# A second batch's attention woven into the first batch's groups: steps planned by a search, and steps from a fixed table

## The chip, the cores and the metric

The kernel runs on one core of one Trainium2 chip. Its metric is the device time of one execution in microseconds (us), the median of several runs. In this text TensorE is PE in the profile (PEld is its weight load), VectorE is DVE, ScalarE is ACT, GpSimd is POOL and SyncE, which issues the DMAs, is SP.

## What is computed

Agent attention for two batches, then a feed-forward layer with a learned slope, cut here to what matters:

```
# q, k, v: (2, 12480, 128); agents: (2, 49, 128)
def sm(a, b):
    s = scale * (a @ b.transpose(0, 2, 1))
    s = s - s.max(-1, keepdims=True)
    e = np.exp(s)
    return e / (e.sum(-1, keepdims=True) + 1e-09)
agent_v = sm(agents, k) @ v            # per batch: needs all keys and values
x = (sm(q, agents) @ agent_v).reshape(24960, 128)
h = x @ w_in                           # w_in: (128, 2048)
g = np.maximum(h, 0) + alpha * np.minimum(h, 0)
out = g @ w_out                        # w_out: (2048, 128)
```

## The kernel before

Queries are taken in 52 groups of 480 (26 a batch), and each group in 8 steps, so there are 416 steps; two groups make a pair of 16 steps. A step s first issues the matmuls of `h` for step s + 2 (`g1`: six, L824, then ScalarE's `rh` = relu, L830, and VectorE's `rl` = the rest that `rh` rounds off, L831), then whatever the plan holds for step s, then twelve matmuls that add `rh` and `rl` into `acc` (`g2`, L846). All are 480 columns wide and use half of the rows each, two side by side. `h` has two buffers, so the matmuls of `h` for step s + 2 overwrite what `rl` of step s reads. `acc` has two banks, one for even and one for odd groups; whatever else TensorE computes during a group (`pair_tile`) uses the bank of the other group, between the read-out of the last group and the start of the next. At the end of a group `acc` goes through `os` (L862, L863), is transposed at the next group's step 1 (`o_take`, L868), scaled (`o_scale`, L873) and stored (`o_store`).

Each pair of groups also has its query chain (`q_transpose` to `q_rec`), on fixed steps, among them the query logits at the pair's step 2 (`q_logits`, L740), GpSimd's all-reduce that follows (`q_max`, L753) and the sums at step 4 (`q_sum`).

The first batch's keys and values are done ahead of step 0. Those of the second batch must be done, and folded with `w_in` into `sab` and with the linear part into `zh`, `zl`, by step 208, where its groups begin; they are woven into the first batch's steps. Keys come in 25 units of 512: a load (`load_kb`, four DMAs on SP), a transposition on VectorE (`kt`, L366), a burst of sixteen small float32 matmuls for two units (`k_logits`, L384), a copy on ScalarE and an addition on VectorE (`k_take`), and a maximum (`k_max_keys`, L423). After all of them `k_max` joins the maxima. Values follow: subtract the maximum (`k_exp_a`, L507), exponentials (`k_exp_b`), the low part (`k_exp_c`, L526), the values' two parts (`v_split`, L497, L498, with a memset on GpSimd), a burst of matmuls (`k_av2`, L572) and an addition (`k_add`, L582). Then the fold: `t1` divides by the denominator, `t2` turns the result, four `ta` multiply it with a quarter of `w_in` each, `tz` and `ts` make `zh` and `zl`.

Before, a search puts all that on steps: `fit` gives VectorE and ScalarE budgets a step (`ROOM`, L21), `hold` finds two free steps for a bank (L1026), and each unit goes to the first step that has room (L1060 to L1119). The code below shows it; the order of the code inside a step is the order of the engines' queues, and each engine takes its queue strictly in that order.

Of the kernel before, what the change touches and what calls it, by code (L numbers as in the profile page):

```python
# [13 lines left out]
ALU = mybir.AluOpType  # L14
# [3 lines left out]
WORD_LO = 2.0**-15  # L18
WORD_HI = 122880.0

ROOM = {"dve": 1.4, "act": 1.1}  # L21


CUTS = (3, 8, 15, 21)
# [7 lines left out]
def kernel(  # L32
# [11 lines left out]
    nc = tc.nc  # L44
    B, N, C = q.shape
# [8 lines left out]
    NG = N // GT  # L54
    KT = 512
    UB = KT // P
    NU = -(-N // KT)
    NKB = NU * UB
    W = 512
# [4 lines left out]
    NM = NF // 2  # L64
# [39 lines left out]
    win = const.tile([P, DFF], F32, name="win")  # L104
# [485 lines left out]
    def fold_tasks(b):  # L590
        w = st[b]

        rows = w["rows"]
        parts = rows // NA
# [31 lines left out]
            t = big(b, "sab", F32R)  # L626
            w["sa"], w["sb"] = t[:, 0:DFF], t[:, DFF : 2 * DFF]

        def ta(n):
            def f():  # L630
                t = pair_tile(f"a_ps{b}_{n}", 0 if b == 0 and n == 1 else None)[:, 0, :]
                sl = slice(n * W, (n + 1) * W)
                nc.tensor.matmul(t, lhsT=w["avt"], rhs=win[:, sl], start=True, stop=True)
                nc.scalar.copy(out=w["sa"][:, sl], in_=t)
                nc.vector.tensor_tensor(
                    out=w["sb"][:, sl], in0=t, in1=w["sa"][:, sl], op=ALU.subtract
                )

            return f

# [58 lines left out]
    NGT = B * NG  # L699
# [193 lines left out]
    with tc.manual_schedule():  # L893
# [7 lines left out]
        for b in range(B):  # L901
# [3 lines left out]
            out=oma, in0=alp, scalar1=-1.0, scalar2=1.0, op0=ALU.mult, op1=ALU.add  # L905
# [7 lines left out]
        def at(s, f, *a):  # L913
            plan.setdefault(s, []).append((f, a))
# [9 lines left out]
        s = 0  # L924
# [78 lines left out]
            at(4, f)  # L1003

        q_steps = (-20, -19, -18, -14, -13, -13, -10, -7, -6, -5, 4, 5, 10)
        load = {}

        first = {}

        def pre(s, f, *a):  # L1010
            first.setdefault(s, []).append((f, a))

        def use(s, eng, cost):
            load[eng, s] = load.get((eng, s), 0.0) + cost

        def fit(s, **costs):

            while any(load.get((e, s), 0.0) + c > ROOM[e] for e, c in costs.items()):
                s += 1
            for e, c in costs.items():  # L1020
                use(s, e, c)
            return s

        busy = set()

        def hold(s):  # L1026

            while s in busy or s + 1 in busy or s % NM in (0, 1, NM - 1):
                s += 1
            busy.update((s, s + 1))  # L1030
            return s

        for i2 in range(NGT // 2):
            s0 = 2 * NM * i2
            if i2 == 0:
                at(10, q_sum, 0)
                pre(11, q_spread, 0)
                at(13, q_rec, 0)
                busy.update((0, 1, 2, 3, 4, 5, 6, 7, 10, 11))
# [6 lines left out]
            for i in (3, 10):  # L1046
                busy.update((s0 + steps[i], s0 + steps[i] + 1))
            for f, i in zip(q_chain, steps):
                (pre if f in (q_take, q_spread) else at)(s0 + i, f, i2)
        for g in range(NGT):  # L1050
            s0 = g * NM
            for i in range(NM):
                use(s0 + i, "dve", 0.57)
            for i in (7, 7, 0, 1):
                use(s0 + i, "act", 0.5)
# [4 lines left out]
        for b in range(1, B):  # L1060
            base = (b - 1) * NG * NM
            parts = [(u, u + 2) for u in range(0, NU - 3, 2)] + [(NU - 3, NU)]
            assert NU % 2
            at(base + 8, k_begin, b, [(0, NU)], parts)
            s = base + 9
            done, used = {}, {}
            for c, (lo, hi) in enumerate([*parts[:-1], (NU - 3, NU - 1), (NU - 1, NU)]):
                us = tuple(range(lo, hi))
                for u in us:
                    s = fit(max(s, done.get(u - 3, 0) + 1), dve=0.57)  # L1070
                    at(max(base, s - 9, used.get(("k", u - 3), 0) + 1), load_kb, b, u)
                    used["k", u] = s
                    at(s, k_transpose_dve, b, u)
                    s += 1
                t_log = hold(max(s + 1, done.get(lo - 1, 0) + 2))
                done.update((u, t_log) for u in us)
                at(t_log, k_logits, b, us)
                pre(t_log + 1, k_take, b, us)
                use(t_log + 1, "dve", 0.4)
                if hi in (NU, *(p[1] for p in parts)):  # L1080
                    t_max = fit(t_log + 2, dve=0.4)
                    at(t_max, k_max_keys, b, min(c, len(parts) - 1))
            s = t_max + 1
            at(s, k_max, b)
            s += 3
            done = {}
            for lo, hi in parts:
                us = list(range(lo, hi))
                t_av = s
                for u in us:  # L1090
                    s = fit(s, dve=0.3)
                    at(s, k_exp_a, b, u)
                    t_v = fit(max(s, done.get(u - 4, 0) + 1), act=0.5, dve=0.57)
                    at(max(base, t_v - 8, used.get(("v", u - 3), 0) + 1), load_v1, b, u)
                    used["v", u] = t_v
                    at(t_v, v_split, b, u)
                    t_e = fit(max(s + 1, done.get(u - 4, 0) + 1), act=0.5)
                    at(t_e, k_exp_b, b, u)
                    t_c = fit(t_e + 1, dve=0.3)
                    at(t_c, k_exp_c, b, u)  # L1100
                    t_av = max(t_av, t_c + 2, t_v + 2)
                t_av = hold(t_av)
                at(t_av, k_av2, b, us)
                pre(t_av + 1, k_add, b, us)
                use(t_av + 1, "dve", 0.5)
                for u in us:
                    done[u] = t_av
            s = t_av + 2
            at(s, k_sum, b)
            lead, rest = fold_tasks(b)  # L1110
            s += 2
            for f in lead:
                s = hold(s)
                at(s, f)
                s += 2
            s = hold(s)
            at(s, rest[0])
            at(s + 1, rest[1])
            s += 2  # L1119
            assert s < base + (NG + 1) * NM - 1, (t_max, t_av, s, base + NG * NM)  # L1120

        for s in range(NS):
            step[0] = s
# [40 lines left out]
```

## Time and profile before

| | us |
|---|---|
| median of 3 runs (lowest, highest) | 1036.93 (1036.47, 1040.59) |
| the profiled execution | 1038.73 |
| its span, first to last instruction | 1037.0 |
| TensorE busy | 1015.8 (98%) |
| VectorE busy | 818.2 (79%) |
| ScalarE busy | 630.5 (61%) |
| GpSimd busy | 112.7 (11%) |

Busy shares are means over stages that differ: the stage ahead of step 0 ends near 92 us, the second batch's work lies between 110 and 600 us, and behind it the groups run alone. Matmuls are pipelined and their ends are modelled, so a wait of TensorE shows first in the starts of its instructions and in its weight loads. What the views name by line is the code above; the names of the tiles stand behind the lines.

### The profile page before, as it was taken

Reading aid. Unit: us, or ns where it says so; the run is one execution under the profiler, and the core shown is the slowest. Engines: PE = TensorE matmul, PEld = TensorE weight load, DVE = VectorE, ACT = ScalarE, POOL = GpSimd, SP = SyncE. Lnnn points to the kernel's source line nnn. Section 1 sums busy time; section 2 is a strip of 40 time slices with the busy share of each in tenths; the row PEclk is TensorE's granted clock in tenths of the full one; section 3 lists DMA queues with packets and bytes.
Section 4 is the critical chain, followed back from the end, with each engine's and each line's share of the span. In section 5 each row is a group of like instructions: output and inputs, shape, how many; then the busy total and the mean of one; then the engine's idle time right before and its main releaser. Section 6 shows DMA issues by size and latency. Waiting matters only on the chain.

```text
span 1037.0 us, 22307 instructions
## 1 busy us (share of the span) xinstructions
PE 1015.8 (98%) x9263; PEld 935.2 (90%) x9263; DVE 818.2 (79%) x1040; ACT 630.5 (61%) x801; POOL 112.7 (11%) x138
## 2 busy tenths in 40 slices
PE   9899999999999999999999999999999999999997
PEld 7786888988988888999888799999999998999997
DVE  6966778878878899988977777787778777887775
ACT  4355556656656576777755665666666665666563
POOL 3341110010011011011011011101110011101100
PEclk9899999999999999999999999999999999999999
DMA  9963034324332222332220211121112111211011
GB/s 297 290 131 50 14 51 67 53 44 67 52 49 36 61 63 59 70 79 54 59 35 12 39 30 19 32 40 30 26 24 39 31 33 19 39 30 21 11 20 30
DMA packets 295045, 57.22 MB, mean 55 GB/s; under 512 B 265567, under 2 KB 292769, under 8 KB 294945
## 3 DMA queue, kind: packets, MB, share of 16 engines
q1 hardware_dynamic: 293953, 55.69, 26.8%
q8 instruction: 72, 1.18, 0.5%
q10 hardware_dynamic: 992, 0.12, 0.1%
q14 instruction: 28, 0.23, 0.1%
HBM read 42.59 MB, written 12.78 MB: 53 GB/s over the span
## 4 chain that ended last, share of the span: by engine, by line
PE 79%; DVE 13%; ACT 3%; issue 2%; DMA 1%; SPq 1%; DVEq 0%; ACTq 0%
PE acc L846 43%; PE h L824 22%; DVE rl L831 4%; PE lg L740 3%; PE kl L384 3%; ACT rh L830 2%; PE av L539 2%; PE acc L857 1%; DVE qt L718 1%; PE qsum L782 1%; DVE ql L730 1%; DMA qin<-in_q_dram 1%; DVE kt L366 1%; PE ktp L352 1%; ACT qh L725 1%
## 5 line engine op out<-in xcount | busy, mean ns | idle before, releaser
L831 DVE SCALAR_TENSOR_TENSOR rl<-h,rh 128x960 fp32r<-128x960 f32 x416 | 478.7, 1152 | 184.4 <-ACT rh L830 181.0
L830 ACT ACTIVATE rh<-h 128x960 fp32r<-128x960 f32 x416 | 404.5, 972 | 288.4 <-PE h L824 282.9
L824 PE MATMUL h<-qmh,sab 64*128 64x480 f32 x1664 | 380.5, 379 | 5.1 <-DVE rl L831 4.3
L846 PE MATMUL acc<-rh,wl 64*128 64x480 f32 x1664 | 379.7, 380 | 1.3 <-DVE zl L649 0.7
L846 PE MATMUL acc<-rh,wh 64*128 64x480 f32 x1664 | 376.9, 377 | 0.0
L846 PE MATMUL acc<-rl,wh 64*128 64x480 f32 x1664 | 294.2, 378 | 0.0
L824 PEld LDWEIGHTS h<-qmh,sab 64*128 64x128 f32 x1664 | 234.6, 184 | 23.7 <-DVE rl L831 10.3
L846 PEld LDWEIGHTS acc<-rh,wl 64*128 64x128 f32 x1664 | 232.4, 184 | 16.8 <-issue 3.8
L846 PEld LDWEIGHTS acc<-rh,wh 64*128 64x128 f32 x1664 | 233.6, 185 | 9.8
L846 PEld LDWEIGHTS acc<-rl,wh 64*128 64x128 f32 x1664 | 203.5, 184 | 10.4
L824 PE MATMUL h<-qml,sab 64*128 64x480 f32 x832 | 204.0, 377 | 0.0
L753 POOL PARTITION_ALL_REDUCE qm<-qs x26 | 79.6, 3063 | 714.3 <-ACT qs L748 694.3
L824 PEld LDWEIGHTS h<-qml,sab 64*128 64x128 f32 x832 | 118.2, 184 | 4.5
L384 PEld LDWEIGHTS kl<-ag,kt 64*128 64x128 f32 (+2 forms) x588 | 50.6, 192 | 2.0 <-issue 0.5
L862 ACT COPY os<-acc 128x480 f32<-128x480 f32 x52 | 29.1, 560 | 37.0 <-PE acc L857 37.0
L384 PE MATMUL kl<-ag,kt 64*128 64x49 f32 (+2 forms) x588 | 51.1, 272 | 0.2 <-ACT kt L356 0.2
L863 DVE TENSOR_TENSOR os<-acc,os 128x480 f32<-128x480 f32 x52 | 33.6, 647 | 2.4 <-ACT os L862 2.4
L725 ACT CAST qh<-qt 128x960 fp32r<-128x960 f32 x26 | 25.9, 996 | 14.6 <-DVE qt L718 14.6
L868 DVE STREAM_TRANSPOSE ot<-os 128x480 f32<-128x480 f32 x52 | 34.7, 667 | 0.0
L873 DVE TENSOR_TENSOR ot<-ot,qr 128x480 f32<-128x480 f32 x52 | 33.7, 647 | 0.0
L404 ACT COPY s<-kl 128x196 f32<-128x196 f32 (+2 forms) x38 | 14.0, 369 | 28.7 <-PE kl L384 28.7
L748 ACT COPY qs<-lg 128x960 f32<-128x960 f32 x26 | 25.0, 960 | 10.5 <-PE lg L740 10.5
(148 smaller groups left out, 873.3 us busy)
## 6 DMA issues: line engine op xcount, KB each, us to landing
qin<-in_q_dram SPq DMA_DIRECT2D x208, 60.0 KB, 2.2
out_dram<-ot SPq DMA_DIRECT2D x206, 60.0 KB, 1.9
v<-in_v_dram SPq DMA_DIRECT2D x12, 512.0 KB, 7.0
kb<-in_k_dram SPq DMA_DIRECT2D x96, 64.0 KB, 2.2
v<-in_v_dram SPq DMA_DIRECT2D x24, 256.0 KB, 2.8
k<-in_k_dram SPq DMA_DIRECT2D x11, 512.0 KB, 8.7
win<-in_moe_w_in_dram SPq DMA_DIRECT2D x4, 512.0 KB, 8.0
wo<-in_moe_w_out_dram SPq DMA_DIRECT2D x4, 512.0 KB, 9.6
```

What stands on the lines that cost most here:

```text
L384: nc.tensor.matmul(d[0:rows, c : c + NA], lhsT=kt[r0:r1, n * rows : (n + 1) * rows], rhs=st[b]["ag"][r0:r1, 0:NA], start=True, stop=True,)
L725: nc.scalar.copy(out=t, in_=gq["t", k])
L740: nc.tensor.matmul(t[:, i, 0:GT], lhsT=a[r0:r1, h].rearrange("p d a -> p (d a)"), rhs=x[r0:r1, h, :], start=n == 0, stop=n == len(jobs) - 1,)
L753: nc.gpsimd.partition_all_reduce(flat(t), flat(gq["s", k]), P, ReduceOp.max)
L824: nc.tensor.matmul(h[:, u, 0:GT], lhsT=w[a][r0:r1, f0 : f0 + P], rhs=x[r0:r1, :], start=n == 0, stop=n == 2,)
L830: nc.scalar.activation(out=rh, in_=h[:, :, 0:GT], func=AF.Relu)
L831: nc.vector.scalar_tensor_tensor(out=rl, in0=h[:, :, 0:GT], scalar=0.0, in1=rh, op0=ALU.max, op1=ALU.subtract)
L846: nc.tensor.matmul(acc[:, i, 0:GT], lhsT=a[r0:r1, 2 * m + u, :], rhs=x[r0:r1, u, :], start=m == 0 and n == 0, stop=False,)
L862: nc.scalar.copy(out=t, in_=acc[:, 0, 0:GT])
L863: nc.vector.tensor_tensor(out=t, in0=acc[:, 1, 0:GT], in1=t, op=ALU.add)
L868: nc.vector.transpose(out=t.rearrange("p t i -> p (t i)"), in_=oo.pop(g))
L873: nc.vector.tensor_tensor(out=t, in0=t, in1=gq.pop(("r", g)).to_broadcast([P, TB, 32]), op=ALU.mult)
```

## The change

The search is gone. Fixed tables give the step of each piece within a pair of groups. Keys: three bursts a pair, at its steps 6, 10 and 12, with their transpositions at 2, 3, 4, 7, 8 and 10, from step 16 on. Values: two bursts a pair, at 6 and 12, from step 96 on. The fold: `t1` at 190, `t2` at 198, two `ta` of two quarters each at 202 and 204 (two bursts in one two-bank tile where there were four), `tz` and `ts` both at 206. `o_scale` and `o_store` of odd groups go to steps 2 and 3 behind the group instead of 7 and 8. Five operations of the second pair's query chain, which run in the first pair, move one step ahead. The same instructions are issued.

```diff
-ROOM = {"dve": 1.4, "act": 1.1}
+KEYS_FROM, VALUES_FROM = 16, 96
+KEYS = (((2, 3), 6, 8), ((4, 7), 10, 12), ((8, 10), 12, 16))
+VALUES = (
+    (((0, 2, 1, 3), (0, 2, 2, 3)), 6),
+    (((3, 4, 4, 5), (3, 8, 6, 8)), 12),
+)
+FOLD = (190, 198, 202, 204, 206, 206)
...
-        first = [t1, t2] + [ta(n) for n in range(4)]
+        whole = [(0, 1), (2, 3)] if b else [(n,) for n in range(4)]
+        first = [t1, t2] + [ta(*ns) for ns in whole]
...
-                steps = (-15, -14, -13, -11, -10, -10, -7, -6, -5, -4, 4, 5, 10)
+                steps = (-15, -14, -14, -11, -10, -10, -8, -7, -6, -5, 4, 5, 10)
...
-            at((g + 1) * NM + 7, o_scale, g)
-            at((g + 1) * NM + 8, o_store, g)
...
+            d = 7 if g % 2 == 0 or g == NGT - 1 else 2
+            at((g + 1) * NM + d, o_scale, g)
+            at((g + 1) * NM + d + 1, o_store, g)
...
+        pieces = [*parts[:-1], (NU - 3, NU - 1), (NU - 1, NU)]
+        for c, (lo, hi) in enumerate(pieces):
+            s0 = KEYS_FROM + c // len(KEYS) * 16
+            turn, log, top = KEYS[c % len(KEYS)]
+            us = tuple(range(lo, hi))
+            for u, s in zip(us, turn):
+                load(load_kb, "k", u, s0 + s)
+                at(s0 + s, k_transpose_dve, 1, u)
+            at(s0 + log, k_logits, 1, us)
+            pre(s0 + log + 1, k_take, 1, us)
+            if hi != NU - 1:
+                at(s0 + top, k_max_keys, 1, min(c, len(parts) - 1))
+            last = s0 + top
+        at(last + 1, k_max, 1)
...
+            s0 = VALUES_FROM + c // len(VALUES) * 16
+            steps, av = VALUES[c % len(VALUES)]
+            us = list(range(lo, hi))
+            for u, (a, x, e, d) in zip(us, (*steps, steps[-1])):
+                at(s0 + a, k_exp_a, 1, u)
+                load(load_v1, "v", u, s0 + x)
+                at(s0 + x, v_split, 1, u)
+                at(s0 + e, k_exp_b, 1, u)
+                at(s0 + d, k_exp_c, 1, u)
+            at(s0 + av, k_av2, 1, us)
+            pre(s0 + av + 1, k_add, 1, us)
```

VectorE's queue from `rl` of step 48, the head of a pair with keys. Names carry the step or group: `rl48`, `ot4` (`o_scale` or `o_take` of group 4), `os5`, `kt1_11` (unit 11), `mx1` (`k_max_keys`). Before:

```order
L831 SCALAR_TENSOR_TENSOR rl48_2618<-h48_2610,rh48_2617 128x960
L730 TENSOR_TENSOR ql4_2621<-qt4_2570,qh4_2595 128x960
L366 STREAM_TRANSPOSE kt1_11_2623<-kb1_5632_2322 128x512
L831 SCALAR_TENSOR_TENSOR rl49_2645<-h49_2637,rh49_2644 128x960
L873 TENSOR_TENSOR ot4_2454<-ot4_2454,qr2_2483 128x480
L366 STREAM_TRANSPOSE kt1_12_2649<-kb1_6144_2498 128x512
L863 TENSOR_TENSOR os5_2666<-acc5_2428,os5_2666 128x480
L831 SCALAR_TENSOR_TENSOR rl50_2677<-h50_2669,rh50_2676 128x960
L831 SCALAR_TENSOR_TENSOR rl51_2710<-h51_2702,rh51_2709 128x960
L868 STREAM_TRANSPOSE ot5_2713<-os5_2666 128x480
```

After:

```order
L845 SCALAR_TENSOR_TENSOR rl48_2649<-h48_2641,rh48_2648 128x960
L744 TENSOR_TENSOR ql4_2652<-qt4_2582,qh4_2627 128x960
L845 SCALAR_TENSOR_TENSOR rl49_2674<-h49_2666,rh49_2673 128x960
L887 TENSOR_TENSOR ot4_2458<-ot4_2458,qr2_2490 128x480
L877 TENSOR_TENSOR os5_2693<-acc5_2432,os5_2693 128x480
L845 SCALAR_TENSOR_TENSOR rl50_2704<-h50_2696,rh50_2703 128x960
L429 TENSOR_REDUCE mx1_1350<-s1_1349 128x49
L845 SCALAR_TENSOR_TENSOR rl51_2733<-h51_2725,rh51_2732 128x960
L882 STREAM_TRANSPOSE ot5_2736<-os5_2693 128x480
L845 SCALAR_TENSOR_TENSOR rl52_2758<-h52_2750,rh52_2757 128x960
L887 TENSOR_TENSOR ot5_2736<-ot5_2736,qr2_2490 128x480
L372 STREAM_TRANSPOSE kt1_12_2775<-kb1_6144_2460 128x512
```

The two transpositions among `rl48` to `rl50` are gone; a maximum stands between `rl50` and `rl51`, the odd group's `o_scale` and a transposition between `rl52` and `rl53`.

VectorE's queue in a pair with values. Before, from `rl142`, where a burst for units 8 and 9 stands at step 142 (`v2_1_9`: the split of unit 9):

```order
L831 SCALAR_TENSOR_TENSOR rl142_5723<-h142_5715,rh142_5722 128x960
L718 STREAM_TRANSPOSE qt10_5726<-qin10_5088 128x960
L498 TENSOR_TENSOR v2_1_9_5728<-v1_9_5430,v2_1_9_5728 128x4x128
L831 SCALAR_TENSOR_TENSOR rl143_5752<-h143_5744,rh143_5751 128x960
L498 TENSOR_TENSOR v2_1_10_5757<-v1_10_5465,v2_1_10_5757 128x4x128
```

After, from `rl132`, step 2 of a pair; `e2_1_8` and the `s1` rows behind `rl133` stand at step 3, as `q_max` does on GpSimd:

```order
L845 SCALAR_TENSOR_TENSOR rl132_5398<-h132_5390,rh132_5397 128x960
L887 TENSOR_TENSOR ot15_5373<-ot15_5373,qr7_5157 128x480
L504 TENSOR_TENSOR v2_1_8_5415<-v1_8_5128,v2_1_8_5415 128x4x128
L504 TENSOR_TENSOR v2_1_9_5419<-v1_9_5130,v2_1_9_5419 128x4x128
L845 SCALAR_TENSOR_TENSOR rl133_5448<-h133_5440,rh133_5447 128x960
L532 TENSOR_TENSOR e2_1_8_5375<-s1_1349,e2_1_8_5375 128x4x49
L532 TENSOR_TENSOR e2_1_9_5423<-s1_1349,e2_1_9_5423 128x4x49
L513 TENSOR_TENSOR s1_1349<-s1_1349,kmax1_1351 128x196 x2
L845 SCALAR_TENSOR_TENSOR rl134_5483<-h134_5475,rh134_5482 128x960
```

Before, unit 9's split stands behind `rl142`, two steps ahead of its burst and behind a query transposition; now the splits of units 8 and 9 stand four steps ahead of their burst, and four instructions that read two tiles each follow one another behind `rl133`.

## Rows read from the trace of the kernel before

**Rows 1.** The page, part 1: TensorE's busy time, share of the span, instructions.
```profile
PE 1015.8 (98%) x9263; PEld 935.2 (90%) x9263; DVE 818.2 (79%) x1040; ACT 630.5 (61%) x801; POOL 112.7 (11%) x138
```

**Rows 2.** The chain of waits in order of time: start us, us, what.
```profile
139.47 1.31 PE lg L740 x12
...
177.76 1.31 PE lg L740 x12
...
519.20 1.31 PE lg L740 x12
...
631.24 1.32 PE lg L740 x12
...
868.35 1.32 PE lg L740 x12
```

**Rows 3.** Waits of TensorE's weight loads, 90 to 640 us: total, times, longest.
```profile
PEld h L824 <- DVE rl L831: 10.3, 16, 1.0
...
PEld acc L846 <- ACT os L862: 1.7, 3, 0.6
PEld acc L846 <- DVE zl L649: 1.1, 1, 1.1
PEld av L572 <- POOL v L501: 1.0, 2, 0.6
```

**Rows 4.** Timeline of TensorE at a key pair's head: start us, us, what [idle before].
```profile
211.99 0.63 PE L846 MATMUL acc<-rl,wh 64*128 64x480 f32 x4
212.43 0.40 PE L824 MATMUL h<-qmh,sab 64*128 64x480 f32 x2
...
213.96 0.62 PE L846 MATMUL acc<-rl,wh 64*128 64x480 f32 x4
215.12 0.48 PE L824 MATMUL h<-qmh,sab 64*128 64x480 f32 x2 [0.53 <-DVE rl L831]
```

**Rows 5.** Timeline of VectorE at the same place.
```profile
212.20 0.64 DVE L873 TENSOR_TENSOR ot<-ot,qr 128x480 f32<-128x480 f32 x1
212.76 0.70 DVE L366 STREAM_TRANSPOSE kt<-kb 128x512 f32<-128x512 f32 x1
213.38 0.62 DVE L863 TENSOR_TENSOR os<-acc,os 128x480 f32<-128x480 f32 x1
213.92 2.20 DVE L831 SCALAR_TENSOR_TENSOR rl<-h,rh 128x960 fp32r<-128x960 f32 x2
```

**Rows 6.** Bursts: key logits on the chain of waits, values in TensorE's timeline.
```profile
149.10 1.72 PE kl L384 x32
150.82 1.37 PE acc L846 x12
...
377.19 1.14 PE L572 MATMUL av<-v,e 64*98 64x258 f32 x16
378.15 0.39 PE L846 MATMUL acc<-rh,wl 64*128 64x480 f32 x2
```

**Rows 7.** Timelines of VectorE and GpSimd behind the same query logits.
```profile
217.08 1.16 DVE L831 SCALAR_TENSOR_TENSOR rl<-h,rh 128x960 fp32r<-128x960 f32 x1 [0.38 <-ACT rh L830]
...
218.44 3.04 POOL L753 PARTITION_ALL_REDUCE qm<-qs  x1 [35.17 <-ACT qs L748]
```

**Rows 8.** Timelines of GpSimd and VectorE around an all-reduce in a value pair.
```profile
407.77 3.04 POOL L753 PARTITION_ALL_REDUCE qm<-qs  x1 [19.99 <-DMA v<-in_v_dram]
...
408.13 1.64 DVE L526 TENSOR_TENSOR e<-s,e 128x196 fp32r<-128x196 f32 x1
409.69 0.35 DVE L507 TENSOR_TENSOR s<-s,kmax 128x196 f32<-128x196 f32 x1
```

**Rows 9.** Groups of instructions, shapes apart: count, busy us, mean ns, idle before.
```profile
L497 ACT CAST v<-v 128x512 fp32r<-128x512 f32 x24 | 14.7, 611 | 0.0
...
L423 DVE TENSOR_REDUCE mx<-s 128x49 f32<-128x392 f32 x12 | 10.2, 848 | 0.0
```

**Rows 10.** Timeline of SP's DMA issues: two key loads of four DMAs each.
```profile
215.46 4.20 SPq L344 DMA_DIRECT2D kb<-in_k_dram  x8
```

More of the change, by code (lines that the diff above doesn't have):

```diff
@@ L627, in t2, with ta @@
             w["sa"], w["sb"] = t[:, 0:DFF], t[:, DFF : 2 * DFF]
-        def ta(n):
+        def ta(*ns):
             def f():
[L631 to L637, printed above, removed]
+                i = 0 if b == 0 and ns == (1,) else None
+                ps = pair_tile(f"a_ps{b}_{ns[0]}", i)
+                for t, n in enumerate(ns):
+                    nc.tensor.matmul(
+                        ps[:, t, :], lhsT=w["avt"], rhs=win[:, n * W : (n + 1) * W],
+                        start=True, stop=True,
+                    )
+                for t, n in enumerate(ns):
+                    sl = slice(n * W, (n + 1) * W)
+                    nc.scalar.copy(out=w["sa"][:, sl], in_=ps[:, t, :])
+                    nc.vector.tensor_tensor(
+                        out=w["sb"][:, sl], in0=ps[:, t, :], in1=w["sa"][:, sl],
+                        op=ALU.subtract,
+                    )
             return f
@@ L1005 @@
         q_steps = (-20, -19, -18, -14, -13, -13, -10, -7, -6, -5, 4, 5, 10)
-        load = {}
         first = {}
@@ L1011, in pre @@
             first.setdefault(s, []).append((f, a))
[L1013 to L1031, printed above, removed]
         for i2 in range(NGT // 2):
@@ L1038 @@
                 at(13, q_rec, 0)
-                busy.update((0, 1, 2, 3, 4, 5, 6, 7, 10, 11))
                 continue
@@ L1042 @@
             if i2 == 1:
-                steps = (-15, -14, -13, -11, -10, -10, -7, -6, -5, -4, 4, 5, 10)
+                steps = (-15, -14, -14, -11, -10, -10, -8, -7, -6, -5, 4, 5, 10)
             else:
                 at(max(0, s0 - 38), q_load, i2)
-            for i in (3, 10):
-                busy.update((s0 + steps[i], s0 + steps[i] + 1))
             for f, i in zip(q_chain, steps):
@@ L1051 @@
             s0 = g * NM
[L1052 to L1055, printed above, removed]
             at((g + 1) * NM + 1, o_take, g)
-            at((g + 1) * NM + 7, o_scale, g)
-            at((g + 1) * NM + 8, o_store, g)
[L1060 to L1120, printed above, removed]
@@ new lines, with load @@
+            d = 7 if g % 2 == 0 or g == NGT - 1 else 2
+            at((g + 1) * NM + d, o_scale, g)
+            at((g + 1) * NM + d + 1, o_store, g)
+        parts = [(u, u + 2) for u in range(0, NU - 3, 2)] + [(NU - 3, NU)]
+        assert B == 2 and NU % 2 and NS // 2 >= KEYS_FROM + 16 * 12
+        at(KEYS_FROM - 8, k_begin, 1, [(0, NU)], parts)
+        used = {}
+        def load(f, what, u, s):
+            at(max(KEYS_FROM - 8, s - 9, used.get((what, u - 3), 0) + 1), f, 1, u)
+            used[what, u] = s
@@ new lines @@
+        at(last + 1, k_max, 1)
+        assert last + 3 < VALUES_FROM
+        for c, (lo, hi) in enumerate(parts):
+            s0 = VALUES_FROM + c // len(VALUES) * 16
[9 more added lines that the diff above has]
+            pre(s0 + av + 1, k_add, 1, us)
+            last = s0 + av + 1
@@ L1122 @@
+        at(last, k_sum, 1)
+        lead, rest = fold_tasks(1)
+        for s, f in zip(FOLD, (*lead, *rest)):
+            at(s, f)
+        assert last < FOLD[0]
         for s in range(NS):
```

## The prediction

> **What bounds the kernel now.** I read the page first: TensorE is busy 98% of the span [rows 1], so time can only come from what TensorE does or from short waits that its busy share hides. A clock for that is the burst of twelve query logits (`q_logits`), which stands once in each pair of groups, at step 2 of 16, on the chain of waits [rows 2]. From 631.24 to 868.35 lie seven pairs without any second-batch work: 237.11 / 7 = 33.87 us a pair, with no wait in them. From 139.47 to 177.76, a pair with keys, it is 38.29. From 139.47 to 631.24 lie 13 pairs: 491.77 us, against 13 x 33.87 = 440.3 without that work. So the second batch's keys, values and fold cost 51.5 us there. The question is how much of it is matmul work, which the change keeps, and how much is waiting.
>
> **Work in it, by bursts.** A burst of key logits (two units) takes 1.72 us and the next accumulating block takes 1.37 where 1.32 is usual: 1.77 [rows 6]. Eleven of them and the last unit (2 blocks of 8, 0.44) give 19.9. A burst of values is 378.15 - 377.19 = 0.96 [rows 6]; eleven and one of three units (1.2) give 11.8. The fold's matmuls (denominator, `avt`, four `a_ps`, `z_ps`) I take at 7.0 by the gaps between such starts in the TensorE timeline: 5.6 for themselves, 0.2 for each of seven changes to plain float32 and back. Sum 38.7. The rest, 51.5 - 38.7 = 12.8, is waiting. A second view says the same: TensorE's weight loads waited 10.3 us for `rl` in 16 places, 1.7 for the accumulator's bank, 1.1 for `zl`, 1.0 for `v` [rows 3], 14.1 in all; loads run ahead of the matmuls, so each counts somewhat more than is lost. Ahead of 139.47 two more places lie in that sum; I put them at 1.2 (0.35 at the first key burst, 0.85 in the next pair's head, as in the place below). Waiting before: 12.8 + 1.2 = 14.0.
>
> **The mechanism of one wait.** The matmuls of `h` at 215.12 could have started about 0.44 after 213.96, as 212.43 did after 211.99; they start 1.16 after, 0.72 late, and run 0.1 long: 0.8 lost [rows 4]. They need the buffer that `rl` at 213.92 reads; it is two steps back. VectorE reached that `rl` late because `o_scale`, a key transposition and the `os` addition stood ahead of it, 212.20 to 213.92 [rows 5]. How late may it be? After `h` at 215.12 the unhindered `rl` starts at 217.08, 1.96 later [rows 4, 7], ends 1.16 after that, and the buffer is wanted two steps of 1.97 after the start: 3.94 - 3.12 = 0.8 us of room. Extra VectorE work between two `rl` is free until it pushes the second more than 0.8 past its input.
>
> **What the change does to that, key pairs.** Instruction counts are the same on every engine (8838 matmul passes, 1042 on VectorE in the built order), so work cancels and places count. I walk VectorE with start-to-start times: an instruction's follower starts 0.08 ahead of its end [rows 5], so `rl` counts 1.07, a transposition 0.62, `o_scale` 0.56 [rows 5], `kmax` 0.77 [rows 9]; read in the timeline in the same way, the addition of key logits 0.47, `o_take` 0.59, `q_rec` 0.75, `q_split` 1.07, `q_transpose` 1.09. Head of the pair, step 2 at 0: `rl` 1.96, `o_scale` 3.03, transposition 3.59 to 4.2; the next `rl` has its input at 5.2 (step 2 lasts 3.28 with the query logits). Nothing is late. The old crowd of steps 14 to 17 has lost its two transpositions. The fullest stretch is steps 8 to 13, step 8 at 0: `rl` 1.96, `kmax` 3.03, transposition 3.80 to 4.42; `rl` 4.42 instead of 3.93 (late 0.49 of 0.8), `o_take` 5.49; `rl` 6.08 instead of 5.90, `q_rec`, transposition, addition until 8.99; the burst at step 10 has put the next input at 9.63. Then `q_split`, `rl` at 11.77 instead of 11.60, and `q_transpose`, `kmax`, addition until 15.17 with the next input at 15.33, for step 12 carries a burst too. So a third burst fits, and lengthens TensorE's pair by its own 1.77: 33.87 + 3 x 1.77 = 39.2 in four pairs, with the waits of 0.8 at each key pair's head gone.
>
> **Value pairs.** Before, bursts fall where `k_add` or a `v` split is still owed (accumulator's bank and `v` in [rows 3]). Now the bursts stand at 6 and 12, two steps or more after their inputs: 33.87 + 1.92 = 35.8 in five pairs. The keys end at step 89 instead of 109, values run from 96 to 189, and the fold's last step is 206 instead of 207.
>
> **What the new order loses.** The odd groups' `o_scale` and store move five steps earlier in all pairs; by the walk above `o_scale` at 3.03 costs nothing also where no keys are. At the end of the keys (steps 88 to 92) `kmax` of three instructions (1.1), `o_take` and `k_max` (1.1) follow one another: late by about 1.4 against 0.8, and again 0.1 some steps on: 0.7. Ahead of the first keys, steps 14 to 18: 0.3. At step 190 the denominator's matmul wants `k_sum`, which VectorE reaches after `rl`: 1.96 + 1.07 + 0.42 = 3.45 after step 189's start, against 1.97 + 0.66 = 2.63: 0.8, and 0.15 to refill. Sum 2.0. `zl` is one step earlier and its wait goes; two bursts of two `a_ps` save two changes of type, 0.3.
> Sum: 14.0 - 2.0 + 0.3 = 12.3 us less. The profiled execution (span 1037.0, 1038.73 in all) would become 1024.7 and 1026.4. It lies 1.8 above the median, 1036.93, which becomes **1024.6**. Bounds: all 14.1 + 1.2 gone and nothing lost, 1021.6; 4 lost in the new order and a base of only 13, 1027.9.
>
> **A rule against the change.** One VectorE subtraction (`e`, from two SBUF tiles) that began 0.36 into GpSimd's all-reduce took 1.64 us and ended 2.0 after the all-reduce began; the next, of the same size, began 1.9 into it and took its usual 0.35 [rows 8]. In value pairs the change puts four such instructions right behind `q_max`. The all-reduce starts 3.3 after step 2's `h` [rows 4, 7], later by what ScalarE now does ahead of it (two casts of 0.61 each [rows 9] and an exponential): 3.3 to 4.8. With the release 2.0 after its start the four (0.27 each) end by 7.9, and the next `rl`, whose input is there at 7.1, is late by 0.8; the room is 1.24 here, since step 4 carries the sum's matmuls. With an earlier start the two `v` splits ahead of them are held instead. I count 0, with 0.3 a pair as the far end.
> The Trainium skill (SBUF — State Buffer, "Who interferes with whom") has it that a VectorE instruction with two SBUF inputs contends with a GpSimd instruction that reads SBUF, and that the later one is blocked until the other is through. By that rule the block lasts all 3.04 us; the trace agrees on the block but shows the release after 2.0.
>
> **Rivals.** *A, as worked out*: 1024.6, its own range 1022 to 1028. *B, the all-reduce holds VectorE to its end*: in six value pairs the four instructions wait until 4.84 + 3.04 = 7.88 and end at 8.97, `rl` is late by 1.83, 0.6 past the room, 0.7 with the refill: 4.2 more, 1028.8. For it: the row of 1.64. Against: the one behind it [rows 8]. The page named above is what this rival follows. *C, half comes back*: the room of 0.8 is eaten by short waits that the walk has no row for (a burst's copy, a queue's delay), 0.5 in each of twelve pairs: 1030.6. Against: the same walk gives the wait of 0.8 at 215.12. *D, slower*: key loads come late. The odd group's store now goes to SP ahead of three key loads; it can't start before `o_scale` ends (3.6), four DMAs take SP 2.1 [rows 10]; the first load is then issued by 7.8 and lands about 2.2 later (the page's median for `kb`), at 10; its transposition stands at step 7, near 16. It decides once loads are 6 late; then VectorE stands still and TensorE loses all but 0.8. To pass 1042 they must be 10 late in four pairs. Nothing in the trace is near that. *E, the order changes nothing*: the built order shows the moves, so only waits that I have put down to the order would have another cause: 1035.
>
> **How the numbers follow.** A 0.68, B 0.14, C 0.12, D 0.03, E 0.03. The prediction is A's. The range goes from 1022 to 1030, over B, and leaves out most of C, D, E and A's edges. About 0.5%, 5.2 us, is what a measurement of this kernel can tell from no change: below 1031.7 lie A, B and three quarters of C, 0.91; within, the rest of C and E, 0.06; slower 0.03.
>
> **What would show it.** In the changed profile key pairs of 39.2 between query-logit bursts, four of them, then value pairs of 35.8; weight loads waiting for `rl` in 3 or 4 places instead of 16, none for `zl` and the accumulator's bank; one wait of about 0.9 at the denominator. Subtractions of 1 us and more behind `qm`, with waits near 0.7 in each value pair, would be B; VectorE idle ahead of `kt` or `qst` would be D; key pairs of 40 and more with `rl` still named, C.

## The result, and the profile after

The changed kernel takes 1025.10 us (median of 5 runs, 1024.42 to 1027.29) against 1036.47 us (median of 5, 1034.14 to 1040.59): 0.9892 of the time before, with a 95% interval of 0.9872 to 0.9912. It is faster, by 11.4 us by the medians; the forecast was 1024.6. The profiled run took 1024.81 us where that of before took 1038.73, so the two profiles differ by 13.9, more than the medians do. To see where, I cut each span at two places: at the first `h` matmuls that step 0 of the main loop issues, and at those that step 224 issues, where the second batch's own work is over in both kernels. TensorE's timeline has the two starts (start us, us, instruction); first the kernel before, then the changed one:

```profile
91.68 0.48 PE L824 MATMUL h<-qmh,sab 64*128 64x480 f32 x2
...
626.46 0.41 PE L824 MATMUL h<-qmh,sab 64*128 64x480 f32 x2
```

```profile
89.28 0.49 PE L838 MATMUL h<-qmh,sab 64*128 64x480 f32 x2
...
612.34 0.37 PE L838 MATMUL h<-qmh,sab 64*128 64x480 f32 x1
```

From step 0 to step 224 it is 534.79 before and 523.07 after: 11.72 less, all of it from the change. Behind step 224 it is 410.49 and 410.67. Ahead of step 0 the profiles differ by 2.40, in code that the change does not touch: the clock granted there is not the same in every run (the last section shows it). Every kernel below is therefore judged by the stretch from step 0 to step 224, read in this way, in which a part that nothing touches repeats within some 0.1 us.

The page, part 1, of the changed kernel, against [rows 1]:

```profile
PE 1007.3 (98%) x9263; PEld 946.7 (93%) x9263; DVE 822.1 (80%) x1040; ACT 630.4 (62%) x801; POOL 116.1 (11%) x138
```

Counts are as before, and so is TensorE's share; its 98% hid the waits in both. The chain of waits shows the bursts of query logits, one in each pair of groups (start us, us, what), against [rows 2]:

```profile
134.54 1.31 PE lg L754 x12
...
173.72 1.31 PE lg L754 x12
...
291.26 1.31 PE lg L754 x12
...
326.18 1.31 PE lg L754 x12
...
505.47 1.31 PE lg L754 x12
...
583.45 1.31 PE lg L754 x12
...
617.30 1.32 PE lg L754 x12
```

From 134.54 to 291.26 lie the four key pairs, 156.72 / 4 = 39.18 each (forecast 39.2). From 326.18 to 505.47 lie five value pairs, 179.29 / 5 = 35.86 (forecast 35.8). From 583.45 a pair without second-batch work takes 33.85. TensorE's weight loads, 90 to 630 us, against [rows 3] (total us, times, longest):

```profile
PEld h L838 <- DVE rl L845: 1.3, 5, 0.5
PEld den L607 <- PE h L838: 1.1, 1, 1.1
```

10.3 us of waiting for `rl` in 16 places have become 1.3 in 5 (forecast in 3 or 4); the waits for `os` (1.7), for `zl` at the accumulator (1.1) and for the ones column of `v` (1.0) are gone; a new one of 1.1 stands at the denominator. The place of [rows 4], the head of a key pair, now reads in TensorE's timeline

```profile
209.65 0.61 PE L860 MATMUL acc<-rl,wh 64*128 64x480 f32 x4
210.09 0.39 PE L838 MATMUL h<-qmh,sab 64*128 64x480 f32 x2
...
211.61 0.63 PE L860 MATMUL acc<-rl,wh 64*128 64x480 f32 x4
212.05 0.41 PE L838 MATMUL h<-qmh,sab 64*128 64x480 f32 x2
```

and VectorE's there, against [rows 5],

```profile
209.12 0.65 DVE L887 TENSOR_TENSOR ot<-ot,qr 128x480 f32<-128x480 f32 x1
209.69 0.65 DVE L877 TENSOR_TENSOR os<-acc,os 128x480 f32<-128x480 f32 x1
210.25 1.15 DVE L845 SCALAR_TENSOR_TENSOR rl<-h,rh 128x960 fp32r<-128x960 f32 x1
```

`h` follows the accumulation by 0.44 both times, where the second was 1.16 before: the key transposition no longer stands between `o_scale` and the `os` addition, and the `rl` whose buffer `h` takes at 212.05 is through at 211.40 (210.25 + 1.15), 0.65 early.

### The profile page after: what moved, and what is told of

Same layout as the page of the kernel before. It is cut to its first block, busy times and chain, and to the rows that moved or that the text cites. A ratio compares the mean times of both kernels' runs of the same rounds, so it can differ in the third digit from the quotient of the medians.

```text
span 1023.0 us, 22323 instructions
## 1 busy us (share of the span) xinstructions
PE 1007.3 (98%) x9263; PEld 946.7 (93%) x9263; DVE 822.1 (80%) x1040; ACT 630.4 (62%) x801; POOL 116.1 (11%) x138
## 4 chain that ended last, share of the span: by engine, by line
PE 95%; DVE 4%; issue 1%; DMA 0%; ACT 0%; SPq 0%; DVEq 0%; ACTq 0%
PE acc L860 53%; PE h L838 26%; PE lg L754 3%; PE kl L390 3%; PE acc L871 2%; PE av L545 2%; PE av L578 1%; PE qsum L796 1%; PE a_ps L640 1%; PE ktp L358 1%; PE warm L166 0%; DVE rl L845 0%; DMA v<-in_v_dram 0%; PE lin_ps L707 0%; DVE mx L429 0%
## 5 line engine op out<-in xcount | busy, mean ns | idle before, releaser
L860 PE MATMUL acc<-rh,wl 64*128 64x480 f32 x1664 | 403.4, 379 | 0.0
L838 PE MATMUL h<-qmh,sab 64*128 64x480 f32 x1664 | 402.3, 378 | 0.9 <-DVE lin L697 0.8
L860 PE MATMUL acc<-rh,wh 64*128 64x480 f32 x1664 | 401.1, 377 | 0.0
L860 PE MATMUL acc<-rl,wh 64*128 64x480 f32 x1664 | 317.0, 378 | 0.0
L838 PEld LDWEIGHTS h<-qmh,sab 64*128 64x128 f32 x1664 | 247.4, 184 | 12.7 <-DVE rl L845 2.1
L860 PEld LDWEIGHTS acc<-rh,wl 64*128 64x128 f32 x1664 | 247.1, 184 | 10.6 <-issue 2.3
L860 PEld LDWEIGHTS acc<-rh,wh 64*128 64x128 f32 x1664 | 248.4, 185 | 7.5
L860 PEld LDWEIGHTS acc<-rl,wh 64*128 64x128 f32 x1664 | 222.8, 184 | 8.4
L838 PE MATMUL h<-qml,sab 64*128 64x480 f32 x832 | 224.9, 377 | 0.0
L732 DVE STREAM_TRANSPOSE qt<-qin 128x960 f32<-128x960 f32 x26 | 30.4, 1170 | 0.2 <-DMA v<-in_v_dram 0.2
```

The costliest lines, as they stand in the source:

```text
L732: nc.vector.transpose(out=flat(t), in_=gq.pop(("in", k)).rearrange("p h t i -> p (h t i)"))
L838: nc.tensor.matmul(h[:, u, 0:GT], lhsT=w[a][r0:r1, f0 : f0 + P], rhs=x[r0:r1, :], start=n == 0, stop=n == 2,)
L860: nc.tensor.matmul(acc[:, i, 0:GT], lhsT=a[r0:r1, 2 * m + u, :], rhs=x[r0:r1, u, :], start=m == 0 and n == 0, stop=False,)
```

## The experiments

Theory: TensorE lost time only where `rl` (or another VectorE result) stood behind too much other work in VectorE's queue; some lateness, about 0.8 us, is free, and what is beyond it is lost. Rivals: VectorE's total load, other causes of the single waits, and the two that the prediction named, B (GpSimd's all-reduce holds VectorE) and C (small waits take half the gain back). All in us; "step 0" is the time ahead of the stretch, "pairs" a full key pair (steps 48 to 64) and a full value pair (steps 144 to 160). In the order of before a key pair holds two bursts and this value pair three; in the changed order it is three and two. So pairs compare only between kernels of the same order; between the two orders the stretch does:

| kernel | step 0 at | steps 0 to 224 | behind | key, value pair | time of that run |
|---|---|---|---|---|---|
| before | 91.68 | 534.79 | 410.49 | 38.28, 37.86 | 1038.73 |
| changed | 89.28 | 523.07 | 410.67 | 39.17, 35.82 | 1024.81 |
| keys alone | 91.90 | 529.48 | 410.50 | 39.18, 37.91 | 1033.69 |
| scale later | 87.14 | 530.03 | 411.67 | 37.71, 37.81 | 1030.62 |
| extra work, step 8 | 91.76 | 529.86 | 410.68 | 40.87, 35.82 | 1034.11 |
| extra work, step 5 | 86.90 | 523.24 | 410.69 | 39.26, 35.82 | 1022.62 |
| hold | 99.85 | 529.61 | 410.68 | 39.18, 36.90 | 1041.94 |
| odd scale back | 87.22 | 523.05 | 410.68 | 39.18, 35.82 | 1022.73 |
| `zl` late | 91.82 | 524.22 | 410.51 | 39.18, 35.82 | 1028.32 |
| burst at 14 | 99.85 | 523.03 | 410.68 | 39.18, 35.81 | 1035.34 |
| burst at 14, split at 12 | 99.81 | 523.18 | 410.67 | 39.17, 35.83 | 1035.45 |
| tail whole | 92.00 | 522.52 | 410.68 | 39.17, 35.82 | 1027.01 |
| two waits mended | 89.86 | 521.70 | 410.68 | 39.17, 35.82 | 1024.04 |
| both | 88.12 | 521.15 | 410.68 | 39.18, 35.82 | 1021.75 |

**Which half of the change pays.** The kernel before with the keys' half (with the key table, the odd groups' `o_scale` at step 2 and the moved query operations of the change):

```
+            pieces = [*parts[:-1], (NU - 3, NU - 1), (NU - 1, NU)]
+            for c, (lo, hi) in enumerate(pieces):
+                s0 = KEYS_FROM + c // len(KEYS) * 16
+                turn, log, top = KEYS[c % len(KEYS)]
...
-            s = t_max + 1
-            at(s, k_max, b)
-            s += 3
+            at(t_max + 1, k_max, b)
+            s = 112
```

> The kernel before with the keys' half of the change alone: the fixed steps for key transpositions, bursts and maxima, the odd groups' o_scale at step 2 and the first pair's q steps; values and fold stay at the steps they have in the kernel before (values from step 112). Measured from the h matmuls of step 0 to those of step 224: 534.8 us in the kernel before, 523.1 in the changed one. Theory (each half of the change ends its own waits for VectorE): key pairs of 39.2, four of them, and about 530 for the stretch, 4.6 less than before; the other 7 belong to values and fold, whose pairs stay at 37.0 to 38.5 as before. Rival (the gain comes from the values' half, three bursts a pair only move the keys' work together): 534 to 535. Rival (nearly all of it is the head of the key pairs): 525 or less.

It took 529.48: 5.31 less than before, so the values and the fold give the other 6.41, by difference: no run has them alone. Key pairs are at once those of the changed kernel; value pairs stay at those of before (38.46, 37.91 and 37.85 for steps 128 to 176). Both rivals fall: neither half is the whole of it.

**Is the wait at the pair's head VectorE's crowd?** The kernel before, one thing moved that the change leaves alone:

```
-            at((g + 1) * NM + 7, o_scale, g)
-            at((g + 1) * NM + 8, o_store, g)
+            d = 9 if g % 2 == 0 else 7
+            at((g + 1) * NM + d, o_scale, g)
+            at((g + 1) * NM + d + 1, o_store, g)
```

> The kernel before with one thing moved that the change does not touch: o_scale and the store of the even groups stand two steps later (step 1 of the next pair instead of step 15), so that VectorE has o_scale, 0.56 us, no longer ahead of the rl that came late in every key pair. Theory (the wait at the pair's head is VectorE's crowd there, and room decides): key pairs 37.7 to 37.8 instead of 38.29, so steps 1 and 2 of a pair together 0.5 shorter, and the stretch of steps 0 to 224 about 530 instead of 534.8. Rival (the wait has another cause, such as the key transposition's own input): pairs of 38.3 and 534.8.

Key pairs took 37.71 and the stretch 530.03, 4.76 less: as expected. 0.56 us of VectorE work that TensorE does not wait for, out of the crowd, gives 0.57 in every key pair. (Behind the stretch this kernel is 1.2 longer, where the last even group's `o_scale` and store now fall among the last group's own.)

**Place or total load?** Four VectorE transpositions more in each of four key pairs, at step 8 or at step 5:

```
+        def extra(i):
+            t = p1m.tile([P, 512], F32, tag="extra", name=f"extra{i}")
+            for n in range(4):
+                nc.vector.transpose(out=t, in_=win[:, n * 512 : (n + 1) * 512])
...
+        for i in range(4):
+            at(KEYS_FROM + 16 * i + 8, extra, i)      # or + 5
```

> The changed kernel with four more VectorE transpositions of 128x512 (0.62 us each, of a constant tile into a tile of their own, nobody waits for them) at step 8 of each of the four full key pairs, the stretch that was worked out as the fullest. Theory (what counts is the place: lateness beyond the room of 0.8 is lost by TensorE): key pairs of 40.6 instead of 39.2, stretch of steps 0 to 224 longer by 5 to 6 us. Rival (only VectorE's total load counts, 80% of the span): no more than with the same work elsewhere. Together with the next run.

> The same four extra transpositions a key pair, at step 5 instead of step 8. Theory (place and room): nothing lost, key pairs 39.2 and the stretch of steps 0 to 224 within 0.5 us of the changed kernel's 523.1. Rival (total load): as much lost as at step 8; with all of the 2.5 us a pair on the path it would be 10 us.

The same work costs 6.79 us at step 8 (1.7 a pair; 5 to 6 in all were expected) and 0.17 at step 5. So the place counts, and VectorE's total load, 80% here, does not. The weight loads' waits of the kernel with the work at step 8, 90 to 640 us, name two places in each pair:

```profile
PEld h L838 <- DVE rl L845: 5.7, 10, 0.9
PEld kl L390 <- DVE s L412: 3.5, 4, 0.9
```

The first is the one worked out (`rl` behind the extra work). The second goes with the part that was lost beyond what I expected: the burst of step 12 waits for its accumulator, which the addition of the key logits of step 10 frees, and that addition was late too. At step 5 the same 2.5 us a pair fit into room that nobody uses.

**Does the all-reduce hold VectorE?** In the changed kernel the subtractions come too late to meet this. The kernel moves four of them ahead of one `rl`:

```
-                at(s0 + a, k_exp_a, 1, u)
+                (pre if a == 3 else at)(s0 + a, k_exp_a, 1, u)
...
-                at(s0 + d, k_exp_c, 1, u)
+                (pre if d == 3 else at)(s0 + d, k_exp_c, 1, u)
```

> The changed kernel with four subtractions of each value pair (two e, two s minus kmax, each with two SBUF tiles as inputs, 0.27 to 0.35 us) moved on VectorE from behind the rl of step 3 to ahead of it, so that the first of them begins some 0.2 to 0.4 us into GpSimd's all-reduce, as the one of 1.64 us did in the kernel before; nothing else moves. Theory (held, and let go 2.0 us after the all-reduce began): the first of the four takes 1.6 to 1.8 us, the rl behind it is late by about 1 us more than the room, value pairs of 36.8 instead of 35.8, the stretch of steps 0 to 224 4 to 6 us longer than 523.1. Rival (held to the all-reduce's end, 3.0): the first takes 2.7, value pairs of 37.8, 10 to 12 us longer. Rival (no hold; the row of 1.64 had another cause): 35.8 and no change.

It took 529.61, 6.54 more, and value pairs of 36.90, 1.08 to 1.16 more in each of six: a little over the 4 to 6 us expected for a release at 2.0, far from the 10 to 12 of a hold to the end. VectorE's timeline and GpSimd's in one such pair:

```profile
376.98 0.69 DVE L504 TENSOR_TENSOR v<-v,v 128x512 fp32r<-128x512 f32 x1
377.58 1.95 DVE L532 TENSOR_TENSOR e<-s,e 128x196 fp32r<-128x196 f32 x1
...
379.72 0.35 DVE L513 TENSOR_TENSOR s<-s,kmax 128x196 f32<-128x196 f32 x1
```

```profile
377.34 3.23 POOL L767 PARTITION_ALL_REDUCE qm<-qs  x1 [28.69 <-ACT qs L762]
```

The first `e` began 0.24 into the all-reduce, took 1.95 us instead of 0.35 and ended 2.19 after the all-reduce began, 1.04 ahead of its end. That is the row of 1.64 in [rows 8] made on purpose, in every pair. The changed kernel at the same place (VectorE, then GpSimd):

```profile
403.44 0.63 DVE L532 TENSOR_TENSOR e<-s,e 128x196 fp32r<-128x196 f32 x2
403.98 0.63 DVE L513 TENSOR_TENSOR s<-s,kmax 128x196 f32<-128x196 f32 x2
```

```profile
401.55 3.22 POOL L767 PARTITION_ALL_REDUCE qm<-qs  x1 [28.70 <-ACT qs L762]
```

Its four subtractions begin 1.89 after the all-reduce's start and take 0.63 two by two: nothing is held. What makes that so is the `rl` that stands ahead of them in VectorE's queue.

**Parts of the change by themselves.** The odd groups' `o_scale` back at step 7 (`d = 7` for all groups), and the fold's last step at 207 again:

> The changed kernel with one part undone: o_scale and store of the odd groups stand at step 7 again instead of step 2. Theory: the room at steps 7 to 8 bears 0.56 us more, stretch of steps 0 to 224 523.1, key pairs 39.2, within 0.3 us; this part of the change is worth nothing by itself. Rival (it made the place for the third key burst): steps 8 and 9 of the key pairs longer by 0.3 to 0.6, 1.5 to 2.5 us in all.

> The changed kernel with the fold's last step one step later, 207 as in the kernel before instead of 206. Theory: the wait of the first accumulation of the second batch for zl comes back at step 208: that step lasts 3.0 instead of 1.97, stretch of steps 0 to 224 longer by 1.0 us. Rival (two bursts of a_ps instead of four, not the step, took that wait away): no change.

The first took 523.05: that move is worth nothing by itself, and the room at steps 7 and 8 bears it. The second took 524.22, 1.15 more: step 208 lasts 3.14, and the wait is back under its own name (weight loads, 90 to 640 us):

```profile
PEld acc L860 <- DVE zl L662: 1.1, 1, 1.1
```

**What made the value bursts wait.** Two kernels, the second value burst at step 14 of five value pairs, with its inputs where they were, or with one `v` split at 12:

```
+            if c % 2 and c < 11:
+                av = 14                                # or
+                steps, av = ((3, 4, 4, 5), (3, 12, 6, 8)), 14
```

> The changed kernel with the second value burst of each full value pair at step 14, where the kernel before had one, instead of step 12; its inputs stay where they are. Theory (not the burst's step costs, only how long its inputs are due ahead of it): value pairs 35.8 and no change of the stretch, within 0.3 us of 523.1. Rival (a burst at step 14 collides with the end of the group, its accumulator's bank and os): 0.5 to 0.7 in each of five pairs, 2.5 to 3.5 us.

> As the kernel before this one (second value burst of a full value pair at step 14, which cost nothing there), but with one of the burst's two v splits at step 12 instead of 8, two steps ahead of the burst, as the splits stood in the kernel before. Theory (the wait comes from a split that VectorE reaches late): a wait at the burst of 0.4 to 0.5, value pairs of 36.3 instead of 35.8, stretch of steps 0 to 224 2.6 us longer than 523.1. Rival (two steps are enough for a split; the kernel before waited for another thing): 523.1 within 0.3.

The burst's step costs nothing (523.03). The late split also cost nothing (523.18), where I had expected 2.6: here my theory failed as I had put it. A split two steps ahead of its burst is early enough, though only just. VectorE's queue shows what was different in the kernel before, at the same step of the same pair:

```profile
465.74 0.30 DVE L526 TENSOR_TENSOR e<-s,e 128x196 fp32r<-128x196 f32 x1
465.95 0.68 DVE L582 TENSOR_TENSOR x<-av,x 98x516 f32<-98x516 f32 x1
...
468.68 0.35 DVE L526 TENSOR_TENSOR e<-s,e 128x196 fp32r<-128x196 f32 x1
...
470.02 1.17 DVE L718 STREAM_TRANSPOSE qt<-qin 128x960 f32<-128x960 f32 x1
471.12 0.65 DVE L498 TENSOR_TENSOR v<-v,v 128x512 fp32r<-128x512 f32 x1
```

Its split ran from 471.12; the burst, begun at 470.93, stood after 8 of its 16 matmuls, since the ones column of `v` on GpSimd waits for the split:

```profile
470.93 0.78 PE L572 MATMUL av<-v,e 64*98 64x258 f32 x8
471.91 0.73 PE L572 MATMUL av<-v,e 64*98 64x258 f32 x8 [0.21 <-POOL v L501]
```

In the kernel with the split at 12 the same two instructions read

```profile
469.32 1.17 DVE L732 STREAM_TRANSPOSE qt<-qin 128x960 f32<-128x960 f32 x1
470.41 0.65 DVE L504 TENSOR_TENSOR v<-v,v 128x512 fp32r<-128x512 f32 x1
```

against a burst that began at 470.79. There the split is done by 471.06, and the burst has its first unit to multiply until about 471.3. Two things I had missed: a burst uses its units one after the other, so the second unit's inputs may be half a burst late; and in the kernel before the split stands behind the `e` subtractions and the addition of the burst before (0.30, 0.68 and 0.35 in the rows above), which put it 0.19 behind the burst's start, where the split at 12 is 0.38 ahead of it. That they are the cause is read from the two queues; no run moves these three by themselves.

The third burst of such a pair costs the kernel before 1.56 to 1.63 (steps 142, 158 and 174) where the two others cost 0.95 to 0.98: some 0.6 is lost. As much again is lost two steps later: steps 144, 160 and 176 are each 0.57 to 0.60 longer than step 0 of a pair without second-batch work. There the next group's first accumulation wants the bank that this burst's addition frees, and VectorE reaches that addition behind two more `e` subtractions (VectorE, then TensorE):

```profile
475.79 0.63 DVE L526 TENSOR_TENSOR e<-s,e 128x196 fp32r<-128x196 f32 x2
476.33 0.69 DVE L582 TENSOR_TENSOR x<-av,x 98x516 f32<-98x516 f32 x1
```

```profile
477.17 0.48 PE L846 MATMUL acc<-rh,wl 64*128 64x480 f32 x2 [0.20 <-DVE x L582]
```

This is the `k_add` still owed that the prediction named. The burst's step is not enough for it: with the burst at 14 in the changed order the pairs keep 35.81.

**A version better than both.** Three losses of the changed kernel, taken out one by one. First the last unit of values, in matmuls of 96 rows instead of 64 and 32:

```
+                if rows < P:
+                    jobs[0].append((e2[0:rows, n, :], v2[0:rows, n, :]))
+                    continue
...
```

> The changed kernel with the last unit of values (two blocks of 96 rows) multiplied as two matmuls of 96 rows instead of four, of 64 and of 32 rows; the burst of three units at step 188 makes its step 2.1 us longer where 1.2 was forecast, and the trace has its last four matmuls 0.29 us apart against 0.12 for the others. Theory (the two halves don't run side by side here, and each change of the number of rows costs time): step 188 shorter by 0.4 to 0.9 and the stretch of steps 0 to 224 with it, 522.2 to 522.7. Rival (the time belongs to the last unit whatever its split, as by a wait for its inputs): no change.

522.52, that is 0.55 less, all at step 188 (3.54 instead of 4.08). TensorE's timelines, first the changed kernel, then this one:

```profile
527.93 2.09 PE L578 MATMUL av<-v,e 64*98 64x258 f32 x20
529.96 0.49 PE L860 MATMUL acc<-rh,wl 64*128 64x480 f32 x2
```

```profile
530.65 1.55 PE L583 MATMUL av<-v,e 64*98 64x258 f32 x18
532.13 0.48 PE L865 MATMUL acc<-rh,wl 64*128 64x480 f32 x2
```

Then the two places at which VectorE was late by the new order itself:

```
-        at(last + 1, k_max, 1)
+        at(last + 5, k_max, 1)
...
-        at(last, k_sum, 1)
+        pre(last, k_sum, 1)
```

> The changed kernel with two of its own losses taken out: k_sum ahead of the rl of step 191 in VectorE's queue (ahead of the denominator's matmul of step 190 there is then 1.1 us less), and k_max four steps later, at step 93 instead of 89, away from the last maxima and the group's end. Theory: the denominator's wait (step 190 lasts 3.18) falls by 0.9 to 1.2, and step 91 (2.42) by 0.4; stretch of steps 0 to 224 1.4 to 1.9 us shorter than 523.1. Rival (k_sum ahead of rl makes the next h late instead; k_max later makes the values late): no gain, 523 or more.

521.70: 1.37 less, just below the 1.4 to 1.9 expected. The denominator, in the changed kernel and in this one:

```profile
534.87 0.30 PE L607 MATMUL den<-x,pair 98*98 98x2 f32 x2 [0.73 <-DVE x L592]
```

```profile
534.06 0.33 PE L607 MATMUL den<-x,pair 98*98 98x2 f32 x2
```

The wait of 0.73 is gone and step 190 lasts 2.41 instead of 3.18, which is 0.77 where 0.9 to 1.2 was expected. The other 0.6 comes from the pair of steps 80 to 96, where `k_max` stood (34.32 instead of 34.71: 0.45 less at step 91, some of it given back at step 95), and from the first value pair (35.85 instead of 36.07). Last, all three together:

> The two mended parts together (k_sum and k_max moved, the last unit's values in matmuls of 96 rows) on the changed kernel. Theory (they lie in different pairs, so they add): stretch of steps 0 to 224 of 521.1 to 521.3 us, 1.9 less than the changed kernel's 523.07 (1.37 and 0.55 apart), and 13.6 less than the kernel before's 534.79; as a ratio to the kernel before 0.985 to 0.989. Rival (the burst's end and the denominator's wait overlap, one hides the other): 521.7, nothing beyond the better one alone.

521.15, so they add up: 1.92 less than the changed kernel and 13.64 less than the kernel before. Timed, it is 1022.27 us (median of 6, 1020.77 to 1033.45) beside 1036.33 for the kernel before (median of 11): 0.9882, with an interval of 0.9844 to 0.9919, wide by the one run of 1033.45, whose mean granted clock of 0.983 is the lowest of the six; `hold`, with step 0 at 99.85, has 0.984. By medians it beats both kernels; its lead over the changed kernel is shown by the stretch alone, of one profiled run each, for the two were not timed side by side.

## Why the prediction was right

Its number holds (1024.6 for 1025.1), and so do its reasons, step by step, with terms that were mis-sized. That it came within 0.5 is in part luck: the gain is 11.4 to 11.5 where 12.3 was forecast, the two largest errors point opposite ways (0.9 and 0.45), and the median of before, with two runs more, is 0.5 lower than the one it started from.

- **The waiting before, 14.0**, was 0.9 too high. What was mis-sized is the value burst of three units: I had 1.2 us, scaled by the number of units, and it takes 2.1 in both kernels, so 0.9 of what I called waiting is matmul work that the change keeps. The last unit has blocks of 96 rows; its matmuls of 64 and 32 rows follow one another by 0.29 us in the trace, while the other sixteen come two by two, 0.12 apart. The tail experiment took 0.55 of it away. The Trainium skill (TensorEngine Tiling (Array Packing), "Key Properties") says that changing the tiling mode drains TensorE. The trace fits that, with 0.29 where the number of rows changes; no run tells such a drain from another reason for which the two sizes do not overlap.
- **The room of 0.8 and the walk of VectorE's queue** hold: pairs of 39.18 and 35.86 where 39.2 and 35.8 were worked out, four key pairs and no wait at their heads; `scale_later` shows that 0.56 us decide there, the two kernels with extra work that the place decides.
- **The new order's losses, 2.0**, measure 1.9: 0.5 around the first key pair (0.3 forecast; steps 13, 14, 17 and 18 of the changed kernel, each 0.10 to 0.16 longer than in later pairs), 0.6 at the maxima, by what moving `k_max` gave back (0.7 forecast), and 0.77 at the denominator (0.95 forecast).
- **The saving by paired `a_ps`, 0.3**, was too small. The four bursts made their steps 5.4 us longer in the kernel before (steps 190, 198, 202 and 204 against the same steps of a pair without second-batch work); the two now do so by 4.4. With `avt` 0.25 longer this is 0.75, by these differences alone: no run undoes the pairing by itself.
- **`zl`** was right: worth 1.15 by itself. **The odd groups' `o_scale`** at nothing was right, 0.02.
- The sum of 12.3 stands against 11.72 in the stretch and 0.18 given back behind it: 11.5. With the measured terms it is 13.1 - 1.9 + 0.75 = 11.95 for the stretch; the 0.2 that are left were not taken apart.
- **Rival B** was rightly left aside, for the reason given: like the second row of [rows 8], the subtractions start 1.89 into an all-reduce of 3.22 and take their usual time, so the hold does not last to its end. (The 2.0 that I took for the release is where the held instruction ended; the last section puts the release near 1.65. The sum is the same, since I counted nothing for it.) The block itself is real, as `hold` shows, at 1.08 us a pair. The Trainium skill (SBUF — State Buffer, "Who interferes with whom") lets the later instruction wait until the other is through. The trace agrees on the block, and shows the blocked instruction through 2.0 to 2.2 us into 3.0 to 3.2. Run only behind the end, `e` would start 1.39 later in each pair of `hold` (3.23 instead of 1.84 into it); by that estimate a pair would have lost more than twice the 1.08.
- **Rival C** (0.5 a pair eaten by small waits) did not come: key pairs of 39.17 to 39.18 and value pairs of 35.82 leave no room for it. Only the first of each kind is longer (39.42 and 36.07), by 0.25, which the losses above already hold. **D**: VectorE never waits for key loads in the changed kernel's trace. **E**, that the order changes nothing, falls with every run here whose only edit is a place.
- Of the values' half the pair's time was right (35.82 for 35.8) and the cause only in part: the wait for `k_add` is there as named, but the splits' steps are not what made the bursts wait, as the failed expectation showed. The queue ahead of them is what the traces point at; that it is the cause was not tested.

## What to carry to other kernels

Where one engine is 98% busy, look for the short waits by comparing the same unit of work with and without the extra part, and ask of each wait how late the awaited instruction may be before it costs anything: work that fits into that room was free here, on an engine busy 80% of the time. When such a schedule is re-ordered, price every burst by its own row, above all the odd-sized last one, and let no estimate scale it by its share. An instruction that another engine can hold may be put behind one that runs anyway, as `rl` here keeps four subtractions out of the part of the all-reduce that would hold them.

## What the runs showed of the hardware

**The clock granted at the start is not the same from run to run.** Ahead of step 0 all kernels here run the same instructions, yet step 0 comes between 86.90 and 99.85 us. TensorE's stretches (us, busy us and matmuls, granted clock, DMA share, GB/s), for the kernel before, the changed one, and `hold`:

```profile
20.00:40.00 20.00, 18.74 (x161) 1.00 1.09 358
40.00:60.00 20.00, 18.10 (x112) 0.74 0.94 205
```

```profile
20.00:40.00 20.00, 17.53 (x151) 1.00 1.09 357
40.00:60.00 20.00, 19.13 (x130) 0.83 0.89 194
```

```profile
20.00:40.00 20.00, 20.00 (x97) 0.50 1.00 324
40.00:60.00 20.00, 18.43 (x149) 0.97 0.79 186
```

At 0.50 of full speed, the lower of its two levels (1.2 of 2.4 GHz), TensorE stays for 20 us in `hold` although it is busy all the time; in `scale_later`, with step 0 at 87.14, the clock is 1.00 throughout these stretches. The 13 us between these extremes are more than the whole change is worth, which is why single runs could not be compared by their time.

**A VectorE instruction that starts first lengthens the all-reduce.** Where a `v` split with two SBUF inputs had begun 0.36 us before it, the all-reduce takes 3.22 or 3.23 us in the rows above, where it took 3.04 in [rows 8]. With `o_scale` begun 0.28 to 0.30 before it, the changed kernel has 3.25 to 3.27; in `scale_later`, where it began 0.18 after a `v` split of 0.68, it took 3.40. In all of these it is longer by what the VectorE instruction still had to run, less some 0.13.

**One that comes behind it is held, and let go at a fixed time of the all-reduce.** Two more cases stand in the traces, an `e` of usually 0.35 in `scale_later` that came 0.93 into the all-reduce, and an `o_scale` of usually 0.65 in `keys_alone` that came 0.36 into it (of each the all-reduce, then the instruction):

```profile
399.10 3.04 POOL L753 PARTITION_ALL_REDUCE qm<-qs  x1 [19.44 <-ACT qs L748]
```

```profile
400.03 1.07 DVE L526 TENSOR_TENSOR e<-s,e 128x196 fp32r<-128x196 f32 x1
```

```profile
402.65 3.04 POOL L755 PARTITION_ALL_REDUCE qm<-qs  x1 [19.88 <-ACT qs L750]
```

```profile
403.01 1.93 DVE L875 TENSOR_TENSOR ot<-ot,qr 128x480 f32<-128x480 f32 x1
```

The first ended 2.00 after the all-reduce began, as that of [rows 8] did, which came 0.36 into it; the second ended 2.29 after. Less their usual times, all three could run from some 1.65 on: an estimate from these rows. In `hold` it is 2.19 - 0.35 = 1.84, in an all-reduce that was itself 0.19 longer.
